# A hand-searched TensorE order is replaced, with longer planned landing times for two kinds of DMA

## Chip, cores and metric

The kernel runs on one core of one Trainium2 chip. The metric is device time in microseconds (us), taken for the whole program; lower is better. Engines are named as in the profile: PE (TensorE matmul), PEld (its weight loads), DVE (VectorE), ACT (ScalarE), POOL (GpSimd) and SP (SyncE, which here only issues DMAs).

## The reference

Two transformer-like layers in a row, each an attention block with a carried memory and a gated feed-forward block, with layer norms without scale ahead of both. Sequence 2048, width 576, 32 heads of 128, segments of 32 tokens, 8 memory tokens, feed-forward width 4608:

```python
for s in range(64):                                  # segments, in order
    h = concat([mem, x[s*32:(s+1)*32]])              # 8 + 32 tokens
    q, k, v = h@Wq, h@Wk, h@Wv                       # 32 heads of 128
    p = softmax(mask(q@k.T * 128**-0.5))             # memory sees all, tokens causal
    o = concat_heads(p@v) @ Wo
    mem, out[s] = o[:8], o[8:]                       # memory carried to the next segment
x = x + A(layernorm(x)); x = x + (silu(n@w1) * (n@w3)) @ w2, n = layernorm(x)
```

The same weights serve both layers. All inputs are bf16.

## The kernel before, in words

The two layers run interleaved, the second `LAG = 8` segments behind the first (L29): step t works on segment t of layer 0 and segment t-8 of layer 1, so there are 72 steps, of which the first 8 and the last 8 have one layer only. A step has four groups g of eight heads. For a group, PE makes Q and K (two units `QK` with tails `QKt`), then scores (`SC`). DVE and ACT make the softmax (mask add, max, subtract, exp on ACT, sum, normalise) and leave the probabilities in a buffer `PB`. They have to be transposed: in two-layer steps a DMA does it (`TR`, L402; the issue is at L1046 to L1050, 112 partitions of 1,024 bf16, 224 times in all), in one-layer steps PE does it (L405, 64 times). The result is in `PTS`, of which there is **one buffer** (`"pts": 1`, L38). PE multiplies it with V (`PV`, L415), the result is copied out to `OT`, and PE multiplies that with Wo (`WO` with tail `WOt`). After the transposition POOL clears `PB` (`pbz`, L406). Eight of the outputs' columns are the memory that the next step's Q, K and V start from.

Between these, PE does the feed-forward block, four segments (128 rows) at a time: up projections `FF` with tails `FFt`, tanh and two multiplications on ACT and DVE, down projections `W2`. The weights of the up projections are loaded from HBM again for each such job, 256 columns at a time (`W13`, L503, four DMAs, 2 buffers), those of the down projections too (`W2l`, L504). All these loads and the transpositions are issued by SP, in one order.

Nothing is scheduled at run time. `make_nodes` (L232) lists 10,997 pieces of work (nodes) with a planned duration, a planned latency `lat` from its end until others may use its result, the buffers that it takes (`acq`) and gives back (`rel`). `plan` (L78) walks through them with a simulated clock, and the order in which it places them is the order of each engine's instructions. For PE the order is not found but given: `FIRST` (L201), `FOUR` (L210, four steps, repeated 11 times) and `LAST` (L214) are strings with one letter for each PE node (Q is `QK`, q its tail, S scores, T a transposition on PE, P `PV`, O and o `WO` and its tail, F and f `FF` and its tail, W and w the down projections of layer 0 and 1, V, G and X the value projections, a small letter their tail). For the rest (the order on DVE, ACT, POOL and SP, whether a copy is done by DVE or ACT, which buffer is taken) the simulated clock decides, so planned durations and latencies matter there. A transposition is planned with 1.27 us of a DMA queue and then `lat`. 

PE can be split into half-width columns or half-height rows; a tail of 64 rows of contraction is done as two row halves at a time. A node that may be done either way (mode `"full/col"`) takes the mode of its neighbours, and in column mode each of its matmuls is written as two of 64 columns (`mm`, L615), which run side by side. Where consecutive nodes have no mode in common, PE changes its mode; the plan counts about 0.1 us for that (L33 to L34).

Of the kernel before, what the change touches and what calls it, by code (L numbers as in the profile page):

```python
# [34 lines left out]
PE_LAT = 0.22  # L35
EW_LAT = 0.135
# [5 lines left out]
def role(t):  # L42

    return (t - LAG) % 2
# [33 lines left out]
def plan(nodes, pools, letters):  # L78


    for n in nodes:
        for d in n.deps:
            d.outs.append(n)
    kinds = {}
    for n in nodes:
        if n.eng == "PE":
            kinds.setdefault(KINDS[n.name], []).append(n)
    its = {k: iter(v) for k, v in kinds.items()}
    seq = [next(its[c]) for c in letters]
    assert len(seq) == sum(len(v) for v in kinds.values())  # L90
    free = {k: [0.0] * c for k, c in pools.items()}
    t_eng = {e: 0.0 for e in ("PE", "ACT", "DVE", "POOL", "DMA", "SWD")}
    ready = {e: [] for e in t_eng}
    both = []
    mode, run = [], []
    order = []

    def settle():
        for x in run:
            x.mode = mode[0]  # L100
        run.clear()
    at = 0

    def push(n):
        if n.eng != "PE":
            (both if n.eng == "AD" else ready[n.eng]).append(n)

    def est(e, n):
        t = max(t_eng[e], n.ready)
        need = {}  # L110
        for s in n.acq:
            if s.i is None:
                need[s.pool] = need.get(s.pool, 0) + 1
        for p, c in need.items():
            t = max(t, sorted(free[p])[c - 1])
        return t

    for n in nodes:
        if n.left == 0:
            push(n)  # L120
    while len(order) < len(nodes):
        best = None
        for e in t_eng:
            if e == "PE":
                cands = seq[at:at + 1] if at < len(seq) and seq[at].left == 0 else []
            else:
                cands = ready[e] + (both if e in ("ACT", "DVE") else [])
            if not cands:
                continue
            ests = [(est(e, n), n) for n in cands]  # L130
            t = min(x for x, _ in ests)
            if t >= NOW:
                continue
            if best is None or t < best[0]:
                best = (t, e, ests)
        if best is None:
            raise RuntimeError(f"the plan is stuck at {at}: {seq[at].name}")
        t, e, ests = best
        st, n = min((x for x in ests if x[0] <= t + 1e-9), key=lambda x: x[1].prio)
        dur = n.dur  # L140
        if isinstance(dur, tuple):
            dur = dur[0] if e == "ACT" else dur[1]
        if e == "PE":
            at += 1
            if not any(m in mode for m in n.mode):
                dur += SWITCHES.get(f"{mode[0]} {n.mode[0]}", SWITCH) if mode else SWITCH
                settle()
                mode = n.mode
            mode = [m for m in mode if m in n.mode]
            run.append(n)  # L150
        elif n.eng == "AD":
            both.remove(n)
        else:
            ready[e].remove(n)
        n.start, n.end, n.by = st, st + dur, e
        t_eng[e] = n.end
        for s in n.acq:
            if s.i is not None:
                continue
            f = free[s.pool]  # L160
            s.i = min((i for i in range(len(f)) if f[i] <= st + 1e-9), key=lambda i: f[i])
            f[s.i] = NOW
        for s in n.rel:
            s.users -= 1
            s.end = max(s.end, n.end + (PE_LAT if e == "PE" else EW_LAT))
            if s.users == 0:
                free[s.pool][s.i] = s.end
        for m in n.outs:
            m.ready = max(m.ready, n.end + (0.0 if m.eng == e == "PE" else n.lat))
            m.left -= 1  # L170
            if m.left == 0:
                push(m)
        order.append(n)
    settle()
    return order
# [20 lines left out]
def ewh(*ns):  # L196
# [2 lines left out]


FIRST = (  # L201
    "amqQqQQSqqQSqQTQQqqSqQSxXVvPTPTOPOoToPOOooQQqqqqQSQvqSQVqQQqQSTqSPTXPOTOPToxoPOOooQQqqqvaSVQQqqQSQqTQPSqQqOSoTPO"
    "TPTPOOoooQQQqqqqQSvSVqqqQQQTSQqPTSOPXTOPTxooPOOooQQpQqqVvqqSnQQSFfqFQqfqqQTQSPFTSfWPOOoofTFPFTOPofOoWQqqqqQQSQQS"
    "FFffqVvqqWQQSTFxqffQFPSXWTFfPOTOPoofTOPFOooWVqfqvQQFSQqqQFSQqfqQWTSQqfPFQTfqFPSOTWPOOFoTooffPFOoWQQqqqqQSvQVSFqf"
    "QqQWqqSQTQPTaOPbSOTxxoPXoTXPOOoovqqpQQQSnQFqfqVSFqfqQQQqSPfqFQfOPSWOPFoOfoFoPWOoFQfqqqQQSQfqFFSGqfgqQQQPWQfqqSFG"
    "SfggGPFOOPWoGogfOPFOooWQQqqfaFSVfqqFQQvqfFSQWQfqqFPSQQWqfOSPFFOoPoWOoffFPOoWQqqqqQQbSQGSQqqgqQQSQqgPGSOPGggOPGOo"
    "PooOoQqqqpQpQQSvqqQSnnVqffFFQQPSqfqFQFSPWwffOFOPwWooFPOOooFqffqQQQqqwWSFQQQqfqfFSGSgqqQQgPGwGPWSggfFOGPOwFPOOooo"
    "oWQqfqqQQQfqSFSVvqqfQQFFPWSfqqQwQFSPaffOwWFPOFOPWOwfooooFfqqQQWQqqSQQqqSbQGgqqSQQgPGSGPGggOPOwOPoooOo"
)
FOUR = (  # L210
    "QQppQqqqqQvVSnnSQFqqfqQQFSqffQPFwOSPWFoffPOFOWwPFOoooFfqfqQQQQqqSWGSFqqfgQQQPQgqqwSGSFPGffggFWGPOwOFPOOoooowVqfq"
    "vQQQQqfqWSFSFfqqqQQwWQFPfqfSFwQOPSWFoFPffOOWPwOoooFqqfQQWQSqqqQQaSbQQqgqqGSQgPGSGPGggOPOwOPoooOo"
)
LAST = (  # L214
    "QqqqpQQQSnpQQqqqVvSnSQfqFFPqfQOWPSwoFffOPFoOFPwOffWooFQQQqqqFQSqffqFQQqgSWGSQPwQqqgfGSFPFgfgGwOPOGOPWOffooooFQQq"
    "qqFSQQqqqVSvQQwWQSPFqfqQOWoPSwFFPffOOWPwOoooFvfqQQQqqqQSVSFfqqfQFQQqqSPWQwSOPVovWPOwOPoobOoXxvppVqqQQQqqSQQnSnqq"
    "QFQSTfqfqQPFSTOPFTOPWTOPwOooooFfqqfQQQSQQqqqVvTSQFQqffqqFSQPwTWPSFfOFTwPOTWPOOooooFqfqfQQQwSQqxvqfXVWSFQFTQfqqWP"
    "wQSTFQfqfqFPSOTwPWFOffOTFPwOoooWoFfqqvVQQQqfqSQWwSFFQfqqQQSTWPQqqOTSoPTOPwOToboPxOoXqqqQQQpSVvqqqQQnSQFTfSFQPfqq"
    "QOTSFfPwOTFPofTOPFOooowQQfqqqQSQFvfqqVSQFfqQQSqfqQTwPFSTFPOTfXxPOTwPOOooooFVqqfvQQQSQqfqqQSQFqqqQSQTwPFTSOPoffTO"
    "FPwTOPoofOoFQQvqqQSQqqVSQqqqQqQSTQPTSPFOOTffooPFTOPwOoopFffFwnwFffffFFFwFwfffFFFwfffFFwFwfffFFFwffFFwfffFFww"  # L220
)
ORDER = FIRST + FOUR * 11 + LAST

# [1 line left out]
class Opt:  # L225

    qk, qkt, sc, tr, pv, wo, wog, vm = 0.0079, -0.0342, 0.0268, 0.1447, 0.0406, 0.2653, 0.0725, 0.1407
# [4 lines left out]
def make_nodes(em, nseg, pools, o=Opt, dma_bw=230e3, load_bw=345e3):  # L232
# [4 lines left out]
    def node(*a, **k):  # L237
        n = Node(*a, **k)
        nodes.append(n)
        return n  # L240
# [5 lines left out]
    kb = lambda rows, cols: rows * cols * 2  # L246
# [108 lines left out]
    def step(t):  # L355
# [3 lines left out]
        e = role(t)  # L359
# [13 lines left out]
        for g in range(NG):  # L373
            qs, qe = [], []
            for u in (2 * g, 2 * g + 1):
# [4 lines left out]
                          prio=pq, mode="full", acq=[q] + b, name="QK")  # L380
                n = node("PE", 4 * mm80, em.qk_tail(t, u, b), deps=hx + hm + ([ld_h[u // 4]] if t == 0 else []), prio=pq + o.qkt, mode="row",
                         acq=[q] + b, name="QKt")
# [6 lines left out]
            s = banks(1)[0]  # L389
            sme = Slot("sme")  # L390
            pf = t + o.gstep * g
# [4 lines left out]
            pb = Slot("pb")  # L396
            d = node("DVE", dve(320) + 0.2, em.sm_sum(t, g, sme), deps=[c], prio=pf, name="sum")
            w = 0.168 * (4 - e if nl == 2 else 2) + nl * 320 / 960
            pbs = node("DVE", w, em.sm_pb(t, g, sme, pb), deps=[d], prio=pf, acq=[pb], rel=[sme], name="pb")
            pts = Slot("pts")  # L400
            if nl == 2:
                tr = node("DMA", 1.27, em.ptr_dma(t, g, pb, pts), deps=[pbs], prio=pf - 0.02, acq=[pts], name="TR", lat=2.0)  # L402
            else:
                bt = banks()
                tr = node("PE", 8 * mm80, em.ptr(t, g, pb, bt), deps=[pbs], prio=pf + o.tr, mode="full/col", acq=[pts] + bt, name="TR")  # L405
            node("POOL", 1.2, em.pb_zero(pb), deps=[tr], prio=pf, rel=[pb], name="pbz")  # L406
            pe_ = [tr] if nl == 2 else [node("AD", ew(4 * c80), em.pt_ev(t, g, m, bt[m], pts), deps=[tr], prio=pf, rel=[bt[m]], name="PTe") for m in (0, 1)]
            if paired(t):
# [6 lines left out]
                      prio=pf + o.pv, mode="full/col", acq=b + [ot], rel=[pts], name="PV")  # L415
# [44 lines left out]
    def job(j):  # L460
# [24 lines left out]
        def units(pps, at0, end):  # L485
            for at, pp in enumerate(pps, at0):
# [3 lines left out]
                for pr_ in (2 * pp, 2 * pp + 1):  # L490
                    prio = (s0 + 4 if end and not last else s0) + o.ff + (o.win if s0 + 4 < nst else o.last_win) * (2 * at + pr_ % 2) / NPR
                    if stays:
                        w13, w2 = kept[pr_]
                        ld = []
                        w2s.append(w2)
                    elif in_tail:
                        w13 = w2 = None
                        ld = tail[pp]
                    else:
                        keep = before_last and pp == npp - 1  # L500
                        w13, w2 = Slot("w13", users=2 + keep), Slot("w2", users=ne + keep)
                        kept[pr_] = w13, w2
                        ld = [node("DMA", kb(1152, 256) / dma_bw, em.load_w13(pr_, w13), prio=prio - 1, acq=[w13], lat=2.0, name="W13")]  # L503
                        lds.append(node("DMA", kb(256, 576) / dma_bw, em.load_w2(pr_, w2), prio=prio - 0.99, acq=[w2], lat=2.0, name="W2l"))  # L504
                        w2s.append(w2)
                    b = banks()
# [863 lines left out]
```

## Time and profile before

| | |
|---|---|
| three runs, us | 2661.4, 2663.74, 2654.18 (median 2661.4) |
| profiled execution, us | 2657.08, of which the span of the instructions is 2655.3 |
| granted PE clock, mean | 0.992 |
| DVE, ACT, POOL busy, us | 2042.0 (77%), 1226.3 (46%), 334.9 (13%) |
| bytes moved by DMA | 371.44 MB, mean 140 GB/s |

The span is made of three stretches by the strings of letters: `FIRST` with the start-up from 12.4 to 528.1 us, 11 periods of `FOUR` up to 2221.1 us, then `LAST`. The profile's idle time of an engine is the time between two of its instructions, and each is put down to the instruction or DMA whose semaphore ended it. "DMA PTS<-PB" is the transposition of the probabilities, "DMA W<-in_B_w_dram" a load of `W13`, "DMA W2C<-in_B_w_dram" one of `W2l`.

### The profile page before, as it was taken

What the parts mean: (1) busy time and instruction counts of PE and PEld (TensorE: products, weight loads), DVE (VectorE), ACT (ScalarE), POOL (GpSimd) and SP (SyncE); (2) the same over time, 40 slices, a digit from 0 to 9 for tenths busy, and PEclk for the clock granted to TensorE, in tenths of its full rate; (3) what the DMA queues carried; (4) which work ended last, traced back from release to release, by engine and by line L of the source; (5) the groups of instructions that cost most, each with busy time, mean ns of one, the idle gap of its engine ahead of it and who ended that gap; (6) DMA issues with size and microseconds to landing.
All of it is one profiled execution on the core that took longest, in us unless ns stands there. A gap on an engine that the chain in (4) does not pass through costs nothing.

```text
span 2655.3 us, 132788 instructions
## 1 busy us (share of the span) xinstructions
PE 2577.3 (97%) x58915; PEld 2226.7 (84%) x58915; DVE 2042.0 (77%) x5253; ACT 1226.3 (46%) x3636; POOL 334.9 (13%) x399
## 2 busy tenths in 40 slices
PE   5999999999999999999999999999999999999998
PEld 4788888888888888888888888888888888888887
DVE  4787787787787778778777787787878777787876
ACT  2555453443445444444544444454534435454453
POOL 1111110110111011011101101110110111011110
PEclk8999999999999999999999999999999999999999
DMA  9064745665665556556454645645464564454456
GB/s 322 4 175 126 194 104 147 126 136 146 128 141 109 142 133 146 139 125 155 117 135 118 161 128 133 158 117 132 116 154 126 134 162 103 127 124 129 128 167 227
DMA packets 683056, 371.44 MB, mean 140 GB/s; under 512 B 233736, under 2 KB 672656, under 8 KB 681840
## 3 DMA queue, kind: packets, MB, share of 16 engines
q1 hardware_dynamic: 678944, 355.07, 52.9%
q8 instruction: 460, 7.54, 1.2%
q0 software_dynamic: 3024, 6.93, 0.9%
q10 hardware_dynamic: 512, 0.94, 0.2%
q14 instruction: 116, 0.95, 0.1%
HBM read 306.72 MB, written 2.36 MB: 116 GB/s over the span
## 4 chain that ended last, share of the span: by engine, by line
PE 83%; DMA 8%; DVE 5%; issue 1%; ACT 1%; SPq 1%; POOL 0%; ACTq 0%; DVEq 0%; POOLq 0%
PE bank L620 83%; DMA PTS<-PB 6%; DVE V L626 1%; DVE STAT L626 1%; DMA W<-in_B_w_dram 1%; DVE HTT L626 1%; DVE PB L626 1%; DVE SME L626 1%; DMA W<-in_A_Wk_dram 1%; SPq L629 1%; DMA W2C<-in_B_w_dram 1%; POOL PB L1041 0%; DMA WV<-in_A_Wv_dram 0%; DVE XR L626 0%; ACT V L623 0%
## 5 line engine op out<-in xcount | busy, mean ns | idle before, releaser
L620 PEld LDWEIGHTS <-W 128*128 128x128 bf16 (+2 forms) x31872 | 1254.5, 100 | 138.0 <-issue 68.5
L620 PE MATMUL bank<-HT,W 128*128 128x80 bf16 (+3 forms) x23040 | 804.6, 197 | 23.1 <-DMA W<-in_A_Wk_dram 8.7
L620 PE MATMUL bank<-XTB,W 128*64 128x256 bf16 (+5 forms) x8832 | 666.8, 263 | 2.5 <-DMA W<-in_B_w_dram 2.0
L1041 POOL MEMSET PB<- 128x1024 bf16 x288 | 274.1, 952 | 1954.7 <-DMA PTS<-PB 1298.5
L623 ACT ACTIVATE QKT<-bank 128x256 bf16<-128x256 f32 (+4 forms) x1546 | 356.3, 315 | 298.1 <-PE bank L620 287.2
L620 PE MATMUL bank<-OT,WO 128*128 128x80 bf16 (+3 forms) x11520 | 413.8, 198 | 1.2 <-ACT OT L623 0.6
L620 PEld LDWEIGHTS <-WO 128*128 128x128 bf16 (+1 forms) x11520 | 385.2, 102 | 26.4 <-issue 13.5
L623 ACT ACTIVATE V<-bank 64x512 bf16<-64x512 f32 (+1 forms) x583 | 328.9, 584 | 129.7 <-PE bank L620 122.5
L620 PE MATMUL bank<-WV,HT 128*32 128x512 bf16 (+3 forms) x3952 | 376.4, 386 | 1.2 <-DVE HT L626 0.7
L620 PE MATMUL bank<-W2C,HTT 128*64 128x288 bf16 (+1 forms) x3032 | 319.1, 287 | 1.3 <-DMA W2C<-in_B_w_dram 1.1
L623 ACT ACTIVATE HTT<-bank 128x512 bf16<-128x512 f32 (+1 forms) x324 | 175.7, 551 | 274.6 <-PE bank L620 273.4
L623 ACT ACTIVATE OT<-bank 128x320 bf16<-128x320 f32 (+1 forms) x378 | 142.2, 402 | 314.9 <-PE bank L620 312.1
L626 DVE TENSOR_REDUCE STAT<-SME 104x8 f32<-104x320 f32 (+1 forms) x576 | 273.6, 475 | 15.7 <-ACT SME L623 9.6
L626 DVE TENSOR_TENSOR PB<-SME,STAT 40x128 bf16<-40x128 f32 (+4 forms) x912 | 274.9, 335 | 11.0 <-DVE STAT L626 0.7
L620 PEld LDWEIGHTS <-HT 128*32 128x32 bf16 (+3 forms) x3952 | 168.3, 102 | 116.5 <-issue 22.1
L626 DVE SCALAR_TENSOR_TENSOR HTT<-HTT,bank 128x512 bf16<-128x512 bf16 (+1 forms) x324 | 202.0, 624 | 77.7 <-ACT HTT L623 74.5
L620 PEld LDWEIGHTS <-HTT 128*64 128x64 bf16 (+1 forms) x3112 | 227.8, 104 | 38.5 <-issue 3.4
L626 DVE SCALAR_TENSOR_TENSOR XR<-bank,XR 128x288 f32<-128x288 f32 x576 | 244.8, 448 | 18.5 <-PE bank L620 14.1
L626 DVE TENSOR_TENSOR HTT<-HTT,bank 128x512 bf16<-128x512 bf16 (+1 forms) x324 | 203.6, 628 | 30.8 <-DVE HTT L626 0.9
L626 DVE CAST V<-bank 64x512 bf16<-64x512 f32 (+1 forms) x281 | 192.2, 684 | 42.7 <-PE bank L620 36.3
L623 ACT ACTIVATE SME<-SME 104x320 f32<-104x320 f32 (+1 forms) x288 | 135.0, 469 | 148.1 <-DVE SME L626 146.4
L626 DVE CAST QKT<-bank 128x192 bf16<-128x192 f32 (+2 forms) x502 | 136.1, 315 | 75.3 <-PE bank L620 73.4
(58 smaller groups left out, 1426.2 us busy)
## 6 DMA issues: line engine op xcount, KB each, us to landing
W<-in_B_w_dram SPq DMA_DIRECT2D x608, 256.0 KB, 3.6
W2C<-in_B_w_dram SPq DMA_DIRECT2D x304, 288.0 KB, 3.5
W<-in_B_w_dram SPq DMA_DIRECT2D x608, 32.0 KB, 3.8
W<-in_B_w_dram SPq DMA_DIRECT2D x8, 1024.0 KB, 13.1
W<-in_A_Wq_dram SPq DMA_DIRECT2D x9, 512.0 KB, 9.2
WO<-in_A_Wo_dram SPq DMA_DIRECT2D x4, 1152.0 KB, 16.7
XR<-in_A_x_dram POOLq DMA_DIRECT2D x16, 288.0 KB, 3.8
WV<-in_B_w_dram SPq DMA_DIRECT2D x4, 1152.0 KB, 9.3
```

The lines of the kernel that those rows point to most:

```text
L620: self.ch("PE", self.nc.tensor.matmul(out, lhsT=lhsT, rhs=rhs, start=start, stop=stop, skip_group_check=True, **k))
L623: self.ch("ACT", self.nc.scalar.activation(*a, **k))
L626: self.ch("DVE", getattr(self.nc.vector, fn_)(*a, **k))
L629: self.ch("SP", self.nc.sync.dma_start(out=out, in_=in_))
L1041: return lambda n: self.ch("POOL", self.nc.gpsimd.memset(self.T.PB[:, pb.i], 0.0))
```

## The change

The three strings are replaced. The kinds of PE nodes and their number stay the same; their order changes. Two planned latencies are longer, and `plan` takes another time at which a buffer that a DMA node gives back is free:

```diff
         for s in n.rel:
             s.users -= 1
-            s.end = max(s.end, n.end + (PE_LAT if e == "PE" else EW_LAT))
+            s.end = max(s.end, n.end + (PE_LAT if e == "PE" else n.lat if e == "DMA" else EW_LAT))
...
-                tr = node("DMA", 1.27, em.ptr_dma(t, g, pb, pts), deps=[pbs], prio=pf - 0.02, acq=[pts], name="TR", lat=2.0)
+                tr = node("DMA", 1.27, em.ptr_dma(t, g, pb, pts), deps=[pbs], prio=pf - 0.02, acq=[pts], name="TR", lat=2.45)
...
-                        ld = [node("DMA", kb(1152, 256) / dma_bw, em.load_w13(pr_, w13), prio=prio - 1, acq=[w13], lat=2.0, name="W13")]
+                        ld = [node("DMA", kb(1152, 256) / dma_bw, em.load_w13(pr_, w13), prio=prio - 1, acq=[w13], lat=2.8, name="W13")]
```

The string of the repeated four steps, before and after (`FIRST` and `LAST` change in the same manner; the first 78 letters of `LAST` stay):

```diff
 FOUR = (
-    "QQppQqqqqQvVSnnSQFqqfqQQFSqffQPFwOSPWFoffPOFOWwPFOoooFfqfqQQQQqqSWGSFqqfgQQQPQgqqwSGSFPGffggFWGPOwOFPOOoooowVqfq"
-    "vQQQQqfqWSFSFfqqqQQwWQFPfqfSFwQOPSWFoFPffOOWPwOoooFqqfQQWQSqqqQQaSbQQgqqGSQgPGSGPGggOPOwOPoooOo"
+    "QqqqqQppQQVvSSnnQqfFQqfFSQQqfqPFOWoPSwFffOPFOwowoWPFOoFfqfQQQQqqqwSWFSGfqgqQQQPQgqqWSSGFPFffggGGPwOOFPOOffWooooFv"
+    "VqqqQQQwSFfqqqQQSwWFSPFfqfqQQOwSPoWFFPffOOwPWOoooFfqqqQWqSaQQQbSQqgqGSQPQqqgGOSPGggoOPGwOPooOo"
 )
```

More of the change, by code (lines that the diff above doesn't have):

```diff
@@ L201 @@
 FIRST = (
[L202 to L206, printed above, removed]
@@ L207 @@
-    "PooOoQqqqpQpQQSvqqQSnnVqffFFQQPSqfqFQFSPWwffOFOPwWooFPOOooFqffqQQQqqwWSFQQQqfqfFSGSgqqQQgPGwGPWSggfFOGPOwFPOOooo"
-    "oWQqfqqQQQfqSFSVvqqfQQFFPWSfqqQwQFSPaffOwWFPOFOPWOwfooooFfqqQQWQqqSQQqqSbQGgqqSQQgPGSGPGggOPOwOPoooOo"
+    "maqQQQqqQqSQQqSqqSqQQTSXxVvPTOPTOPTooOPOooQQqqqqQSQVvSqqQqQQqQTSSPTXPOTOPToxoPOOooQQqqvaSVqqQQQSQTqqqQSPQqTSPOTO"
+    "PTOPoooOoQQQqqqqQSvSVqqQqQQTSQqPTSOPXTOPTxooPOOooQQpvqVqqqQSnQFSfQFqqqfQTQQPSFfqTOSPWFTOoPffFTOPWOoooQQqqqqQSQFS"
+    "FQqfvfVQqqWQTSFPqfTQFPfSWTXxfPOFTOPOOfFooooWVvqqQQQfqqSFQFQSqfqQWTQSqfPFTQqPFSfWTOPOFOoTooffPFOoWQqqqqQQSvQVSfFQ"
@@ L209 @@
+    "qqQWqSQTQPTqOPSbaOoTXPoxTOPxoOoXvpQqqqQQSnQFqfVSQFqfqQQPqSFfqQFSPWOOPooffOWFPoOoFQQqqfQqfqFSWQQqqfgQSFGSGPQFqqgf"
+    "QOPoSGgfWOPFFfgGOPWOoooFQqfqfQQSFQqqfWFSvVFfqqQQQSPqWqQffPSFOaoOPWFOFPoofOoWQQqqqqQSQQbSQqqgqGSQPQqgGSOPgGGPOOog"
+    "oPoOoQqqqppQQQSvqqQnSnVqffFQFPSQQqfqFWFPwSOOffPooFOwFPWOooFffqqQQwQSWQFqqqfQQSFfqqgGSQPQqgWGSwPFfgfgGGPFOOPOOooo"
+    "owQWFQqfqfFSvVqqQwQQWSFqfqqQQPSWfqFQOPSwFFPoffOOWPwOoooFfqqqQQWqSaQQQbSQqgqGSQPQgqqGOSPGgGPgOwOPoooOo"
 )
 FOUR = (
-    "QQppQqqqqQvVSnnSQFqqfqQQFSqffQPFwOSPWFoffPOFOWwPFOoooFfqfqQQQQqqSWGSFqqfgQQQPQgqqwSGSFPGffggFWGPOwOFPOOoooowVqfq"
@@ L212 @@
-    "vQQQQqfqWSFSFfqqqQQwWQFPfqfSFwQOPSWFoFPffOOWPwOoooFqqfQQWQSqqqQQaSbQQqgqqGSQgPGSGPGggOPOwOPoooOo"
+    "QqqqqQppQQVvSSnnQqfFQqfFSQQqfqPFOWoPSwFffOPFOowoWPFOoFfqfQQQQqqqwSWFSGfqgqQQQPQqgqWSSGFPFffggGGPwOOFPOOffWooooFv"
+    "VqqqQQQwSFfqqqQQQSwWFSPFfqfqQQOwSPoWFFPffOOwPWOoooFfqqqQQWqSaQQQbSQqgqGSQPQqqgGOSPGggoOPGwOPooOo"
 )
 LAST = (
-    "QqqqpQQQSnpQQqqqVvSnSQfqFFPqfQOWPSwoFffOPFoOFPwOffWooFQQQqqqFQSqffqFQQqgSWGSQPwQqqgfGSFPFgfgGwOPOGOPWOffooooFQQq"
-    "qqFSQQqqqVSvQQwWQSPFqfqQOWoPSwFFPffOOWPwOoooFvfqQQQqqqQSVSFfqqfQFQQqqSPWQwSOPVovWPOwOPoobOoXxvppVqqQQQqqSQQnSnqq"
@@ L217 @@
[L217 to L220, printed above, removed]
+    "QqqqpQQQSnpQQqqqVvSnSQfqFFPqfQOWPSwoFffOPFoOFPwOffWooFQQQqqqFQSqffqFQQqgSWGSQPQwqqgfGSFPFgfgGwOPOGOPWOffooooFQQq"
@@ new lines @@
+    "qqFSQQqqqVSvQwQWQSPFqfqQOWoPSwFFPffOOWPwOoooFvqqQQQqfqQSVSFfqqfQFQQqqSPWQwSOPVvWPwoOOPoobOoXxvppVqqQQQSqqQQnSnqq"
+    "QFSTqfQQPfqFSTOPFTOPWTOPwOooooFfqfqQQQSQQvqqqVSTFQQqfqfqFSPQWwTSFfOPFTWPOTOPwOooooFfqfqQQQSQxvqqXVFwWSQTffqqFQPw"
+    "SWTQPQFfqfqFOTwSPWFOffOTFPwOoooWoFfqqvVQQQqfqSQWwSFFQfqqQQSTWPQqqOTSoPTOPwOToboPxOoXqqqQQQpSVvqqqQQnSQFTfSFQPfqq"
+    "QOTSoPfFOTwPFTOPoofOoFQQqqqfQQSFvqfqVwSQFfqQQTSfqqFPQTwSFPOTfxXPOTOPFOoooowVvfqQQqqQSQqQSQqfqFqqTQSQPwOTSFPoffTO"
+    "FPwTOPOoooFQqqfqQQSQvqqqVSQQQSqQqfTwPSTOPFTFPOOTffooPFoOopfwFnwFffffFFFwFFfwffFFwffFFwffFFwfffFFwFwFffffFFww"
```

## The prediction

> **What bounds the kernel now.** I read the page's first part, its chain, PE's waits, then single waits. PE is the bound: it is busy for 97% of the span, and no other engine for more than 77%.
>
> ```profile
> PE 2577.3 (97%) x58915; PEld 2226.7 (84%) x58915; DVE 2042.0 (77%) x5253; ACT 1226.3 (46%) x3636; POOL 334.9 (13%) x399
> ...
> PE 83%; DMA 8%; DVE 5%; issue 1%; ACT 1%; SPq 1%; POOL 0%; ACTq 0%; DVEq 0%; POOLq 0%
> ```
>
> The chain gives 8% to DMAs, but a chain is followed back over the whole landing of a transfer, while PE worked for most of it. What PE lost is in the list of waits:
>
> ```profile
> PE bank L620 <- DMA PTS<-PB: 19.9, 29, 1.5
> ...
> PE bank L620 <- DMA W<-in_A_Wk_dram: 8.7, 8, 1.3
> ...
> PE bank L620 <- ACT HT L623: 7.3, 18, 1.6
> ...
> PE bank L620 <- DMA W<-in_B_w_dram: 2.0, 5, 1.0
> ```
>
> The columns are us in total, times, longest. The transpositions are the largest: 15.5 of the 19.9 us lie in the 11 periods, 3.5 in FIRST, 0.9 in LAST. Wk belongs to the start-up. This list counts from the modelled end of a matmul. Counted from when the next could have started (the usual distance of starts), the 224 PVs behind transpositions lost 27.2 us.
>
> One wait shows how. SP's issues, then the chain of waits over it:
>
> ```profile
> 1163.62 2.28 SPq L629 DMA_DIRECT2D W<-in_B_w_dram  x4
> 1166.19 1.24 SPq L1050 DMA_TRANSPOSE PTS<-PB  x1
> 1167.53 1.04 SPq L629 DMA_DIRECT2D W2C<-in_B_w_dram  x2
> 1168.62 2.89 SPq L629 DMA_DIRECT2D W<-in_B_w_dram  x4
> ```
> ```profile
> 1166.19 4.82 DMA PTS<-PB
> 1171.01 0.04 issue
> 1171.06 8.96 PE bank L620 x141
> ```
>
> The last matmul of the PV before started at 1165.91; 0.28 us later, with PTS free, the transposition was issued. It took 4.82 us among weight loads. PE had 3.47 us of other work, and waited 1.6. All transpositions:
>
> ```profile
> DMA to landing us min/median/max: 2.9/3.2/5.2
> ```
>
> The upper quartile is 3.73 us. With no load issued from 2.5 us before to 1.5 us after, the median is 2.94 (58 of them); with 600 KB or more, 3.92 (23).
>
> **The change part by part.** *The free-time rule* does nothing: none of the nodes on the planned DMA queue gives a buffer back (PTS is given back by PV, PB by POOL, W13 by FF; stores are on the other queue). Cost 0, from the code alone, and no wait is added by it.
>
> *The two latencies* move no PE instruction, since its order is the strings'. They change what the simulated clock does on the other engines. ACT's listed order has 59 rows fewer; 55 copies of Q and K more go to DVE (334, before 279), 35 copies of V fewer (VGe 102, before 137). At 315 ns a Q or K piece (two a copy) and 684 ns a V copy that is at most 55 x 2 x 0.315 - 35 x 0.684 = +11 us for DVE in the span, about 0.5% of its load, hidden by its 23% idle time, unless it falls into a softmax: then at most the 11 us come on the path, at least 0. I take 0. On SP 304 W13 loads, 304 W2 loads and 224 transpositions stay; transpositions with a load right ahead fall from 170 to 171, that is, not; right behind, from 181 to 171. POOL's clears keep their order. So the traffic next to a transposition, its cause of lateness, stays.
>
> *More mode changes.* Counting the strings' nodes with their modes: 1,155 mode changes before, 1,238 after: FIRST +11, each period +6 (59 to 65), LAST +6. Starts of consecutive matmuls give the price: full after full 36 ns (1,202 node boundaries, median), row after full 134 (187), column after full 132 (181), full after row 131 (245) against 33 for row after row. So 0.097 us each: 83 x 0.097 = **+8.0 us**, on PE, with nothing to hide it. The order has 868 matmuls more, all halves of column mode; they run in pairs: an FF node takes 1.73 us in columns and 1.75 in full, W2 0.96 and 0.98, VG 1.73 both, PV 0.28 both. I take 0.
>
> *The distances.* I lay the trace's node durations (without waits) along both strings, and measure how much PE work stands between one PV and the next (the time for PTS to be filled again), and between a group's scores and its PV. Of the 224:
>
> | PE work from PV to PV, us | before | waited, us | after |
> |---|---|---|---|
> | under 3.5 | 41 | 14.5 | 4 |
> | 3.5 to 4 | 26 | 2.9 | 39 |
> | 4 to 6 | 61 | 7.1 | 85 |
> | over 6 | 96 | 2.7 | 96 |
>
> At the mean wait of each class of before (in quarter-us steps below 4) the new counts give 18.7 us, **8.5 less**. The other measure says less: scores to PV has 12 groups under 8.5 us, where there were 2, and its classes give 28.7 us, 1.5 more. So the ends are a saving of all 27.2 and a loss of 1.5. Going by place: the third group of steps 32, 36 ... 56 had 3.47 us to the PV before and 10.4 to its scores, and lost 7.1 us in 7 places; it gets 4.73 and 12.73: a landing as at 1166 (4.82 + 0.28) would then cost 0.4, not 1.6. Groups of steps 54 to 59, 15 and 19 with 6.6 us get a longer distance by one measure or the other; I give them 4. Against that, the last group of every fourth step has 8.39 us from its scores, and scores to landing took 8.5 (5% of all) to 9.5 (25%): 0.1 to 1.1 us for 12 groups that lost 2.5 before. I take no change there, and -10 us in all.
>
> By a rule of the Trainium skill (DMA: Bandwidth & Descriptors, sections "Anatomy of one DMA" and "Latency and other measured facts") a DMA has about 2.0 us of fixed cost and a transposition moves up to 261 GB/s; 229 KB here is then, as an estimate from that page, 2.9 us. The trace's undisturbed 2.94 agrees; by it alone the old plan of 1.27 + 2.0 had enough already, nothing would be saved, and the sum would be the +8.0; the trace's upper quartile of 3.73 speaks for the change.
>
> *Longer W13 loads.* PE's waits on W and W2C after the start-up were 2.0 and 1.1 us. At best 3.1 saved, at worst as much again lost. I take -1.
>
> *Others.* The waits on HT (one per period, 0.41 us) stay: the distance of 0.1 us is in both strings. Tails of Q and K come as soon as 1.34 us after the last WOt, before 1.83; the chain over ACT and DVE took 1.15 from that WOt, so 0. Copies of V before a PV have 1.48 us, before 1.89, and a copy takes 0.58 to 0.68: up to 0.3 us in 22 places; I take +1. The start-up waits for weights to about 59 us in either order: 0.
>
> **Sum**: +8.0 - 10 - 1 + 1 = -2 us on the profiled execution's 2657.08: **2655 us**. That execution is 4 us under the median of the three runs, which spread over 9.6; the forecast is no change that can be measured.
>
> **Rivals.** *A, the waits go.* With every PTS wait above 0.3 us a place gone (29 places, -24) and loads never late (-3), the sum is +8 - 24 - 3 = -19: **2638**. For it: the 41 short distances fall to 4. Against it: the traffic beside the transpositions stays, and 5 to 6 us of distance still lost 4.3 us in 8 of 27 places.
>
> *B, only the mode changes show.* If the waits move from PTS to the softmax, as the distance from scores measures it, +8 stays: **2665**, within 0.5%. The page's figures would end here too. Against it: the seven third groups gain on both measures.
>
> *C, slower: the softmax chain takes over.* In the last group of every fourth step and in others near 9 us, DVE (five of the chain's steps) is late, by the extra copies or by their new place. Price: scores to landing at the 50% row of 10.3 us against 8.39 is 1.9 us in 12 groups, 23 us; with 8 for mode changes and 10 saved at the other places, +21: **2678**. It decides from a mean of 9.8 us in these groups on (12 x 1.4 + 8 - 10 = 15). For it: 77% DVE and copies moved to it. Against it: with little distance the chain has hurried, since its order is planned around that: at 8.99 us (step 34) there was no wait.
>
> *D, the change doesn't do what it says*: true of the rule for free buffers, which moves nothing, and priced above.
>
> **Numbers.** Forecast 0.47, A 0.27, B 0.14, C 0.12. The measurement tells 0.5% (13 us) from no change. Faster by over 0.5% is A: 0.27; slower is C with 0.03 of B's edge: 0.15; the rest 0.58. The range goes from just below A, 2635, to 2673, short of C's price and past B's; the unknown ends (-27 to +1.5, -3 to +3, 0 to +11) fill it.
>
> **What would show it.** Right: the wait PE <- PTS at about 8 to 12 us, its third groups without waits, PE busy near 2585, periods at about 153.7 us (before: 153.9 on average, best 152.2). Wrong: PTS waits over 20 us (B or C; in C with the DVE write of PB ending within 3.3 us of PV), or under 4 (A); a busy time of PE that does not rise would say that mode changes are hidden; a landing median off 3.2 us, that SP's order changed the traffic.

## The result and the profile after

The changed kernel takes **2665.76 us** (median of 20 runs, 2660.23 to 2672.33), the kernel before, beside it, 2655.61 (20 runs): ratio 1.0036, 95% interval 1.0028 to 1.0045. So it is 10 us or 0.36% slower, where 2 us faster had been forecast. The number is nearly that of rival B (2665); whether B's reason is the right one is another question.

The profiled execution took 2666.47 us (span 2664.7). Its page, engines' busy time and the chain by engine:

```profile
PE 2589.4 (97%) x59783; PEld 2232.1 (84%) x59783; DVE 2024.0 (76%) x5276; ACT 1253.7 (47%) x3613; POOL 336.0 (13%) x399
...
PE 77%; DMA 5%; DVE 2%; issue 1%; ACT 1%; SPq 1%; POOL 0%; DVEq 0%; POOLq 0%; ACTq 0%
```

PE is still the bound; it is busy for 12.1 us more (2577.3 before) and has the 868 matmuls more that the strings give. The waits of PE in the same kernel (us in total, times, longest):

```profile
PE bank L620 <- issue: 14.5, 14, 3.8
PE bank L620 <- DMA PTS<-PB: 13.8, 22, 1.5
PE bank L620 <- DMA XTB<-in_A_mem_dram: 10.1, 1, 10.1
PE bank L620 <- ACT HT L623: 7.9, 19, 1.9
PE bank L620 <- DMA W<-in_A_Wk_dram: 6.8, 5, 2.6
...
PE bank L620 <- DMA W<-in_B_w_dram: 2.3, 6, 0.9
PE bank L620 <- DMA W2C<-in_B_w_dram: 1.9, 3, 0.9
```

The waits for transpositions did fall, 19.9 to 13.8 us (in the periods 15.5 to 7.5, in FIRST up from 3.5 to 5.4). "Issue", where PE waits for nothing that the profile shows, rose from 8.2 to 14.5; in before it was

```profile
PE bank L620 <- issue: 8.2, 9, 2.9
```

The landing of the transpositions in the kernel after:

```profile
DMA to landing us min/median/max: 2.9/3.1/5.1
```

It is as before (2.9/3.2/5.2). To see where the 10 us lie I cut each span at the first weight load of FOUR and of LAST (weight loads are counted, none is missing in these traces; the ends at 528.1 and 2221.1 us that were given for before ahead are 1.6 to 1.7 us later than this mark):

| us, profiled | to the end of FIRST | FOUR x 11 | LAST to the end | span |
|---|---|---|---|---|
| before | 526.5 | 1692.9 | 435.9 | 2655.3 |
| after | 530.6 | 1689.6 | 444.6 | 2664.7 |

The repeated part became 3.3 us shorter (153.6 us a period, 153.7 had been named as the sign), FIRST 4.1 longer, LAST 8.7 longer. That is one execution of each, and single executions scatter: that of e7 below took 2651.44 us where the median of its kernel is 2661.10.

### The profile page after: what moved, and what is told of

Read it like the earlier page. It is cut to its first block, busy times and chain, and to the rows that moved or that the text cites. A ratio compares the mean times of both kernels' runs of the same rounds, so it can differ in the third digit from the quotient of the medians.

```text
span 2664.7 us, 134355 instructions
## 1 busy us (share of the span) xinstructions
PE 2589.4 (97%) x59783; PEld 2232.1 (84%) x59783; DVE 2024.0 (76%) x5276; ACT 1253.7 (47%) x3613; POOL 336.0 (13%) x399
## 4 chain that ended last, share of the span: by engine, by line
PE 77%; DMA 5%; DVE 2%; issue 1%; ACT 1%; SPq 1%; POOL 0%; DVEq 0%; POOLq 0%; ACTq 0%
PE bank L620 77%; DMA PTS<-PB 4%; DMA W<-in_B_w_dram 1%; DVE STAT L626 0%; DVE V L626 0%; DVE PB L626 0%; DMA W2C<-in_B_w_dram 0%; SPq L1050 0%; DVE SME L626 0%; DVE XR L626 0%; DVE QKT L626 0%; SPq L629 0%; DVE LNS L626 0%; ACT V L623 0%; ACT QKT L623 0%
## 5 line engine op out<-in xcount | busy, mean ns | idle before, releaser
L620 PEld LDWEIGHTS <-W 128*128 128x128 bf16 (+2 forms) x32608 | 1272.0, 101 | 127.3 <-issue 59.7
L623 ACT ACTIVATE QKT<-bank 128x64 bf16<-128x64 f32 (+4 forms) x1440 | 335.6, 310 | 287.1 <-PE bank L620 277.6
L620 PE MATMUL bank<-OT,WO 128*128 128x80 bf16 (+2 forms) x11520 | 418.4, 199 | 6.9 <-issue 5.7
L623 ACT ACTIVATE V<-bank 64x512 bf16<-64x512 f32 (+1 forms) x628 | 353.4, 585 | 122.8 <-PE bank L620 115.6
L620 PE MATMUL bank<-WV,HT 128*32 128x512 bf16 (+4 forms) x3680 | 370.3, 385 | 0.4 <-issue 0.3
L620 PEld LDWEIGHTS <-HT 128*32 128x32 bf16 (+4 forms) x3680 | 159.5, 100 | 135.5 <-issue 31.5
L626 DVE CAST QKT<-bank 128x128 bf16<-128x128 f32 (+2 forms) x608 | 162.7, 315 | 99.8 <-PE bank L620 97.2
L626 DVE CAST V<-bank 32x512 bf16<-32x512 f32 (+1 forms) x236 | 161.4, 684 | 35.2 <-PE bank L620 31.5
```

Source lines behind the costliest of these rows:

```text
L620: self.ch("PE", self.nc.tensor.matmul(out, lhsT=lhsT, rhs=rhs, start=start, stop=stop, skip_group_check=True, **k))
L623: self.ch("ACT", self.nc.scalar.activation(*a, **k))
L626: self.ch("DVE", getattr(self.nc.vector, fn_)(*a, **k))
```

## The experiments

Verdicts are ratios of timed runs to the kernel before on the same chip. "New" and "old" strings are those after and before the change.

**e1 to e4, the parts.** All have the new latencies and the new rule; e1 has the new `FIRST`, e2 the new `FOUR`, e3 the new `LAST`, the other strings old; e4 has old strings only. What e4 keeps of the change:

```diff
-                tr = node("DMA", 1.27, ..., name="TR", lat=2.0)
+                tr = node("DMA", 1.27, ..., name="TR", lat=2.45)
...
-                        ld = [node("DMA", ..., lat=2.0, name="W13")]
+                        ld = [node("DMA", ..., lat=2.8, name="W13")]
```

> The new FIRST string, with FOUR and LAST of before, and the new latencies. Theory by place (the profiles of before and after differ by +4 us in FIRST, -3 in the periods, +9 in LAST and the end, since waits were removed in the periods alone): +4 us on before. Rival (the loss is the 83 mode changes wherever they stand, 0.097 us each, and the waits' sum stays): 11 of the changes are here, +1 us.

Measured: 2665.48, ratio 1.0042 (1.0028 to 1.0056).

> The new FOUR string, with FIRST and LAST of before, and the new latencies. Theory by place: -3 us on before (66 mode changes cost 6.4, waits for transpositions give back 9.6). Rival (mode changes alone): +6 us.

Measured: 2659.68, 1.0016 (1.0007 to 1.0026).

> The new LAST string, with FIRST and FOUR of before, and the new latencies. Theory by place: +8 us on before, with PE's idle time put down to issue in the last 100 us of the span near 9.5 us (before 6.1). Rival (mode changes alone, 6 of them here): +0.6 us, idle time as before.

Measured: 2659.74, 1.0018 (1.0007 to 1.0028).

> The two longer latencies and the free-time rule, with all three strings of before: PE's order is that of before. Theory by place: 0 +- 2 us, and PE's wait for transpositions stays near 20 us. Rival (the other engines' new order is what costs): +5 us or more.

Measured: 2656.69, 1.0008 (0.9999 to 1.0018).

The latencies and the rule cost nothing that can be told, 0 to 5 us. e1, e2 and e3, each one new string with the latencies, cost 10.7, 4.9 and 4.9 us (medians less 2654.82), where +4, -3 and +8 had been expected: all three expectations by place missed. Less the 1.9 us of e4 in each they are 15 us together, where the whole change costs 8 by the same count. The parts don't seem to add up (each ratio is good to some 3 us), as if something were at work that belongs to none of them. e1 also hints at it: it changes nothing in FOUR and yet is as slow as the whole.

**e5, the price of a mode change.** The order of before, with three PVs a period forced to column mode between neighbours of the full mode:

```diff
+            k = at - len(FIRST)
+            if 0 <= k < 11 * len(FOUR) and k % len(FOUR) in (30, 76, 100):
+                em.mode = "col"
```

> Before, with 33 PVs of the periods (three in each) written in column mode between neighbours in full mode: 66 mode changes more, every engine's order as before. Theory: a mode change is on PE and nothing hides it, so 66 x 0.097 = +6.4 us, all of it in the periods. Rival (PE's waits nearby become shorter by as much): 0 to +2 us.

Measured: 2662.34, 1.0021 (1.0012 to 1.0030), that is +5.6 us (3.2 to 8.0) for 66 mode changes, where 66 x 0.097 is 6.4. Its page and its wait for transpositions:

```profile
PE 2584.0 (97%) x59160; PEld 2230.2 (84%) x59179; DVE 2042.4 (77%) x5253; ACT 1226.9 (46%) x3636; POOL 334.7 (13%) x399
```
```profile
PE bank L620 <- DMA PTS<-PB: 17.8, 29, 1.4
```

PE is busy for 6.7 us more than in before (of 59,179 matmuls 19 are not in the trace), and the wait fell by 2.1 only. By the busy time the price stands. The timed 5.6 us agree with it, but prove less: each period has 24 matmuls more here, which moves the instruction fetches that e12 to e18 are about.

**e6 and e7, the large loads near the end.** In the last steps eight large loads of weights (20 DMAs of up to 1,152 KB) come in. Here they load 16 of 128 partitions, in the old (e6) and the new kernel (e7), so the last segments are computed with wrong weights.

```diff
-  self.dma(t13[:, 4 * kind:4 * kind + 4], wd[0:4 * P, fa:fa + 1024].rearrange(...))
+  self.dma(t13[0:16, 4 * kind:4 * kind + 4], wd[0:4 * P, fa:fa + 1024].rearrange(...)[0:16])
...
-  self.dma(t2, self.a.w2[fa:fa + 1024, :].rearrange(...))
+  self.dma(t2[0:16], self.a.w2[fa:fa + 1024, :].rearrange(...)[0:16])
```

> Before, with the eight big weight loads at the end reduced to 16 of their 128 partitions (the last down and up projections then work on wrong weights). Theory (PE's idle time put down to issue near 2590 to 2605 us is its instructions arriving late beside these loads): that idle time of 6.1 us goes to under 1, and the time falls by 5 to 6 us. Rival (those waits have another cause): no change.

Measured: 2652.39, 0.9990 (0.9982 to 0.9999).

> After, with the same eight loads reduced to 16 of 128 partitions (weights of the last job wrong). Theory: the idle time put down to issue in the last 130 us, 11.2 us, goes to under 1, and the time falls by 9 to 10 us, so that after and before with small tail loads are 6 to 7 us apart (before 10). Rival: no change, still 10 apart.

Measured: 2661.10, 1.0018 (1.0007 to 1.0029).

Each became 3 to 5 us faster, so the two are still 8.7 us apart by their medians (7.4 by the ratios): the loads explain some 1.4 to 2.2 of the 10 us, within what these runs can tell. (In the profiles they matter more for the new kernel: its issue waits in LAST fall from 11.5 to 2.4 us, those of the old from 6.3 to 2.5. The timed runs decide.)

**e8, the start.** The new kernel with the first 41 letters of the old `FIRST`:

```diff
-    "maqQQQqqQqSQQqSqqSqQQTSXxVvPTOPTOPTooOPO...
+    "amqQqQQSqqQSqQTQQqqSqQSxXVvPTPTOPOoToPOO...
```

> After, with the first 41 letters (step 0, while the weights arrive) of before. Theory by place: step 0 ends 1 to 1.5 us earlier, as in before, and the time falls by as much; the rest of FIRST stays. Rival (the start does not count, since the next steps wait for loads anyway): no change in the end of FIRST.

Measured: 2664.39, 1.0033 (1.0022 to 1.0044). In the profile step 0 ended 1.6 us sooner than in after, as expected; the whole gained 0.8 to 1.4, less than this measurement tells. The start isn't the cause.

**e9 and e10, the weight traffic.** After the first load of each buffer, W13 and W2 loads are cut to 16 of 128 partitions (stale weights are multiplied), in the old (e9) and the new kernel (e10):

```diff
+            r = 16 if ("w13", w13.i) in self.tail_w else P
-                self.dma(W[:, 4 * kind:4 * kind + 4], wd[0:4 * P, fa:fa + 2 * P].rearrange(...))
+                self.dma(W[0:r, 4 * kind:4 * kind + 4], wd[0:4 * P, fa:fa + 2 * P].rearrange(...)[0:r])
...
```

The rows of 64 and the W2 loads are cut in the same manner.

> Before, with the up and down projections' weight loads reduced to 16 of 128 partitions after each buffer's first (the feed-forward works on stale weights). Theory (transpositions are late because of the weight traffic): their median goes from 3.2 to about 2.95 us and the longest under 4, PE's waits for them in the periods (9.6 to 15.5 us in five profiles with the old FOUR) to under 4, and the time falls by 12 to 18 us. Rival (late for another reason, such as SP's order or the softmax): waits and time stay within 5 us.

Measured: 2644.28, 0.9927 (0.9913 to 0.9940), with the wait of its profile:

```profile
PE bank L620 <- DMA PTS<-PB: 24.2, 29, 1.7
```

> After, with the same loads reduced. Theory: here the waits in the periods go from 7 to under 3 us, so the time falls by 6 to 10 us only, and after stands 14 to 18 us over before, since the 83 mode changes stay (8 us) and there is little left that longer distances save. Rival (the longer distances are worth nothing in any case): both fall by the same, and stay 10 us apart.

Measured: 2651.41, 0.9955 (0.9941 to 0.9970), and

```profile
PE bank L620 <- DMA PTS<-PB: 15.2, 16, 1.9
```

The kernels get 19 and, from 1.0036 to 0.9955, 22 us faster, but not where I had said: the waits for transpositions rose a little in both (19.9 to 24.2, 13.8 to 15.2). Where the 19 us lie I did not follow further; the profiles show 9.8 of them (this chip's runs of the kernel before are some 8 us longer than those of the others, and it has no profile of before), 3.4 in FIRST, 2.8 in the periods, 3.7 in LAST. They are not waits: PE was not busy for 78.0 us of the span in before and 78.6 in e9, while its busy time went from 2577.3 to 2566.9. **My explanation of late transpositions by weight loads fell here.** The two are still 7.1 us apart.

So I looked for what else runs beside a late transposition. The kernel before, third part of its page (queue, kind: packets, MB, share of the DMA engines' time):

```profile
q8 instruction: 460, 7.54, 1.2%
```

7.54 MB in 460 packets is 16.4 KB each, and 58,915 matmuls over 460 is one packet per 128 matmuls with their weight loads (after: 467 for 59,783). So I read these packets as TensorE's instructions, fetched by DMA, and the place of a fetch is a place in the order of matmuls, not in time. The transposition of the prediction's example, issued at 1166.19, had one such fetch in its 4.82 us, at 2.77 us. A transposition raises its semaphore in sixteen steps, and in the trace fifteen of them had come by 3.26 us and the last at 4.82. The DMA view of that stretch:

```profile
q1 hardware_dynamic: 2065, 1.09, 88.2%
q8 instruction: 1, 0.02, 1.2%
```

One, two and three periods later the same transposition took 4.69, 4.70 and 4.56 us, with a fetch at 2.68, 2.51 and 2.13 us: a period of before has 3,330 matmuls, 26.02 fetches, so the same groups are hit period after period (a period of after has 3,410, 26.64, and every third repeats). Over all profiles of this study, with one fetch near and none of another engine:

| fetch starts, us after the transposition's issue | count | landing: quarter, median, three quarters |
|---|---|---|
| none near | 514 | 2.93, 2.97, 3.00 |
| -1.5 to 0 | 614 | 2.91, 2.95, 3.02 |
| 0 to 0.4 | 367 | 2.97, 3.17, 3.31 |
| 0.4 to 0.8 | 388 | 3.33, 3.45, 3.65 |
| 0.8 to 1.2 | 288 | 3.83, 4.01, 4.22 |
| 1.2 to 1.6 | 103 | 4.08, 4.30, 4.53 |
| 1.6 to 2.0 | 64 | 4.37, 4.49, 4.59 |
| 2.0 to 2.4 | 278 | 2.98, 4.40, 4.57 |
| 2.4 to 2.8 | 293 | 2.97, 4.55, 4.70 |
| 2.8 to 4.4 | 409 | 2.91, 2.94, 2.98 |

Transpositions with a fetch in their run land later, by up to 1.6 us in the medians; one that comes when they have landed does nothing. From 2.0 us on, at least a quarter of them are not late at all (2.98). This is a coincidence counted over traces; e12 to e18 below move it on purpose. In e9, with 1/8 of this weight traffic, it is the same: 52 transpositions with a fetch at 0.8 to 2.8 us have a median of 4.42, 140 with none from 0 to 2.8 us 2.91.

**e11, the new strings with the old latencies.** That is the change without the two `lat` and without the rule.

> The three new strings with the old latencies. Theory (the strings make the time; the latencies alone gave +2 +- 2.5): within 3 us of after, so +8 to +12 us on before. Rival (new strings need the other engines' order planned with long latencies): +15 us or more.

Measured: 2672.37 (before on this chip 2663.45), 1.0035 (1.0022 to 1.0047): the strings alone cost all of it.

**e12 to e18, the place of the fetches.** If it is a cause, then a few more matmuls at the start-up, where PE waits for weights anyway, move every later fetch to another place in an order that is otherwise the same, and 128 of them, a whole fetch, move it back onto itself. The added ones are 8 columns wide and their results are not used (60, 128, 32, 96 in the kernel before, 24, 56, 88 in the one after):

```diff
+            for _ in range(60):
+                self.mm(self.bk(b)[:, 256:264], self.T.ident[:, 0:P], self.T.ident[:, 0:8], True, True)
```

> Before, with 60 small matmuls (8 columns, result unused) behind the first one of the start-up, where PE waits some 6 us for weights. All else keeps its order. Theory (a transposition is late when one of PE's instruction fetches, one for each 128 matmuls, falls 0.2 to 2.8 us behind its issue): each later fetch comes 60 matmuls earlier in the work, and laying the shifted fetches on the trace of before gives 37 us of waits for transpositions where unshifted ones give 23: +10 to +14 us. Rival (fetches have nothing to do with it): 0 to +2 us.

Measured: 2663.38, 1.0031 (1.0019 to 1.0043). Two of its waits, which were 19.9 and 1.1 us in before:

```profile
PE bank L620 <- DMA PTS<-PB: 24.8, 34, 1.7
...
PE bank L620 <- DMA W2C<-in_B_w_dram: 4.7, 8, 1.4
```

> The same with 128 small matmuls, a whole fetch. Theory: the fetches fall where they fell, so the time is that of before within 2 us, and the late transpositions are those of before. Rival (the matmuls themselves cost time): twice what 60 cost.

Measured: 2655.39, 1.0000 (0.9990 to 1.0010), with

```profile
PE bank L620 <- DMA PTS<-PB: 17.9, 30, 1.4
```

> The same with 32 small matmuls. Theory: the shifted fetches give 24 us of waits: within 3 us of before. Rival (the matmuls themselves cost time): half of what 60 cost.

Measured: 2661.29, 1.0025 (1.0013 to 1.0037). I had expected within 3 us; it is 5.5 to 6.6.

> After, with 24 small matmuls in the same place. Theory: 20 us of waits where unshifted fetches give 10, so +5 to +10 us on after, +15 to +20 on before. Rival (longer distances keep any late landing hidden): after's time within 2 us.

Measured: 2661.12, 1.0019 (1.0009 to 1.0029): some 5 us *faster* than the changed kernel, where I had expected slower. My model, which moved the fetches of one trace along and added up the lateness, can't forecast the sign; it has the size.

> The changed kernel with 56 small unused matmuls at the start-up, so that every later instruction fetch comes 56 matmuls sooner in the order. At offsets 0 and 24 it was 10 and 5 us above the kernel before. If the order itself costs its 8 us of mode changes less some 6 of waits and the rest of the loss is the place of the fetches, offsets differ by 5 to 8 us and this one may come out as low as 1 to 3 us above the kernel before (2657 to 2659). If the loss is the order's own (mode changes and the softmax chain), it stays at 6 to 12 us above (2662 to 2668).

Measured: 2660.26, 1.0016 (1.0007 to 1.0025), 4.2 us above: between the two expectations.

> The same with 88 matmuls, the fourth offset of about a quarter of a fetch. Mean of the four offsets of the changed kernel: by the place of the fetches at most 5 us above the mean of the four offsets of the kernel before (which is some 4 us above its own time as it stands); by the order's own cost 8 or more above that mean.

Measured: 2659.44, 1.0009 (1.0001 to 1.0018).

> The kernel before with 96 small unused matmuls at the start-up. At 32 and 60 it lost 5 and 7 us, at 128 nothing. If the place of the fetches is what costs, this offset too lies above the kernel as it stands, by 0 to 8 us, or it shows that about half of all offsets are as good as the one it has. If the added matmuls themselves cost time, it would be some 10 us.

Measured: 2658.69, 1.0010 (1.0001 to 1.0019).

In the kernel before, a hundred and twenty-eight matmuls cost nothing and 60 cost 8 us (+10 to +14 had been expected): it isn't the matmuls, it is where they put the fetches. In e12 the two waits shown rose by 4.9 + 3.6 = 8.5 us, which is the whole loss (8.7 between the two profiles, and 8.5 longer periods).

The traces also show it transposition by transposition. From before to e12, 53 of the 224 lose a fetch at 0.8 to 2.8 us behind their issue, and their median landing goes from 4.09 to 3.03 us; 82 gain one, from 3.00 to 4.31; 88 have none in either, 3.04 and 2.99. With a whole fetch added (e13), 46 of the 54 that had one keep it, and stay at 4.20 and 4.29. So the fetch is the cause of the late landing.

All eight, with the wait for transpositions from each profile and the stages as in the first table:

| order, added | us over before (by ratio) | PTS waits, us | end of FIRST | FOUR x 11 | LAST |
|---|---|---|---|---|---|
| old, 0 | 0 | 19.9 | 526.5 | 1692.9 | 435.9 |
| old, 32 | 6.6 | 22.8 | 527.0 | 1699.0 | 432.7 |
| old, 60 | 8.2 | 24.8 | 528.9 | 1701.4 | 433.7 |
| old, 96 | 2.7 | 25.8 | 528.6 | 1696.2 | 437.1 |
| **mean** | **4.4** | **23.3** | **527.8** | **1697.4** | **434.9** |
| new, 0 | 9.6 | 13.8 | 530.6 | 1689.6 | 444.6 |
| new, 24 | 5.0 | 10.4 | 522.3 | 1687.6 | 443.8 |
| new, 56 | 4.2 | 11.6 | 522.0 | 1694.5 | 441.7 |
| new, 88 | 2.4 | 13.1 | 527.8 | 1693.4 | 437.3 |
| **mean** | **5.3** | **12.2** | **525.7** | **1691.3** | **441.9** |

At the same place of the fetches, on average over four, the new order is 0.9 us slower than the old one; with intervals of some 2.6 us on each ratio that is 1 us give or take 2, for these four places. The kernel before has the best of its four, the changed one the worst of its four, so about 9 of the 10 us hang on the places that these two happen to have. For the old order's share, 4.4, the cause is shown: 128 added matmuls do nothing, and in e12 the waits rose as much as the time. For the new order's, 4.3, it is not: no run has 128 matmuls added to the kernel after, its waits for transpositions at its own place are but 1 to 3 us higher than at the other three, and in the profiles its gain lies in FIRST (8 us at 24 and 56) or LAST (7 us at 88), not in the periods. The waits for transpositions are lower in the new order at every place.

The eight profiles also let the sum be redone as a mean. From the old order to the new, PE's busy time goes from 2576.5 to 2584.0 us, 7.5 more, and the rest of the span from 83.5 to 74.8, 8.7 less (19 matmul records are missing in each shifted profile of the old order and 41 in each of the new, which count as idle).

## Why the prediction was wrong

- **The bound**: right. PE, in both.
- **The free-time rule and the latencies, 0**: right within what can be told (e4: 0 to 5 us; e11 without them is no better than the whole change). The working under it was not: the copies of Q, K and V moved with the strings (the latencies alone, e4, move 2 copies of Q and K to DVE, not 55), copies of other kinds moved the other way, and DVE's busy time fell by 18.0 us where up to +11 had been reckoned.
- **Mode changes, +8.0**: right. e5 gave 5.6 (3.2 to 8.0) for 66, expected 6.4, and its PE is busy 6.7 us longer. In the whole change PE's busy time rose by 12.1, 4 more than they give; as a mean of four profiles each it is 7.5. So the 4 belong to this pair. Up to 2.7 of them can be the granted clock, 0.9919 and 0.9909 as the means of the two traces; the rest stays open.
- **The distances, -10**: right as a mean, wrong for the case at hand. On the profiles shown it was -6.1, from 19.9 to 13.8, outside the 8 to 12 that I had set as the sign; over four places of the fetches it is 23.3 to 12.2, -11.1. The third groups of steps 32 to 56 lost their waits as foreseen; others got them, since every third period of after repeats its own pattern of fetches.
- **"So the traffic next to a transposition, its cause of lateness, stays"**: this step failed. Transpositions come late where a fetch of TensorE's instructions falls into them, with 1/8 of the weight traffic as with all of it (e9: 4.42 with a fetch, 2.91 without), and the place of these fetches does not stay when the order changes. I had carried the lateness of each class of distances from the old order to the new; of the classes' mean waits a part was the old order's own luck, and I gave that no price. It is worth 8 us from one place to another without any change in the order (e12), as much as the largest cost of the sum.
- **New waits, +1, start-up, 0, and FIRST and LAST by their mode changes alone**: the waits for copies of V did not grow (2.9 us before, 2.7 after). The start-up was 0.7 us longer in the two profiles, and as long on average (head of the order to its 41st node: 57.5 and 57.6 over the four places). FIRST is 2.0 shorter as a mean. LAST was mis-sized: 0.6 for six mode changes, +7.0 measured as a mean of four profiles, most of it in its last 65 us. The string is not all of it: with the old LAST and the new latencies (e1, e2, e4) LAST took 439.6 to 442.2 us in the profiles, against 432.7 to 437.8 with the old latencies (before, e12, e13, e14, e18); the new LAST with the old latencies (e11) took 442.8. At the end one-layer steps run matmuls of 40 columns, and PE waits for nothing that the profile names. The timeline of PE in the kernel after, start, length, and the wait in brackets:

```profile
2600.08 1.43 PE L620 MATMUL bank<-HT,W 128*128 128x40 bf16 x51 [1.95 <-issue]
2605.74 0.33 PE L620 MATMUL bank<-PTS,V 128*128 128x40 bf16 x7 [1.21 <-issue]
2612.03 1.36 PE L620 MATMUL bank<-OT,WO 128*128 128x40 bf16 x48 [1.46 <-issue]
2619.27 1.75 PE L620 MATMUL bank<-OT,WO 128*64 128x40 bf16 x48 [3.83 <-issue]
```

  In before the same stretch has three such waits, one of 1.36 us at 2589.81 and these:

```profile
2597.12 2.40 PE L620 MATMUL bank<-HT,W 64*128 64x40 bf16 x79 [2.90 <-issue]
2603.33 0.41 PE L620 MATMUL bank<-PTS,V 128*128 128x40 bf16 x7 [1.83 <-issue]
```

  In 2.4 us PE goes through 79 matmuls there, so a fetch of 128 lasts for some 4 us. The traces tell what PE waits for: its next instructions. In after the last six such waits stand at weight loads 58,541, 58,669, 58,797, 58,925, 59,052 and 59,179, that is a fetch apart, and in all twenty profiles the 103 waits of over 0.2 us put down to issue in LAST end 2.2 to 3.6 us (median 2.5) after a fetch started. Over the four places they make 5.1 us in the old order and 8.1 in the new, 3 of the 7.0. Why the fetches come too late just there is not shown: cutting the large loads beside them (e7) shortened LAST to 430.7 us in the profile, but the timed runs gained 4.8 us where the old kernel gained 2.7 (e6), a difference within their intervals.
- **W13 loads, -1**: not seen. W and W2C waits went from 3.1 to 4.2 us; e12 shows that these, too, depend on the place of the fetches (W2C 1.1 to 4.7).
- **Rival B** had the number, not the reason: the waits did not move from PTS to the softmax (the wait for `PB` is 1.9 us, 3 times). **C**: no. **A**: the traffic stayed, and so did a part of the waits. **D**: true of the rule.

What stays open: why the new order at its own place is 5 us slower than at the next three, though its waits for transpositions are but 1 to 3 us higher there (the added matmuls also let step 0 end 1.7 to 2.6 us sooner in their profiles; e8 tells that this alone gives little). One rival was not tested: the granted clock. Its mean over the timed runs is 0.9916 in the changed kernel and 0.9924, 0.9929 and 0.9932 with 24, 56 and 88 matmuls added; the kernel before has 0.9929. From run to run of one kernel 0.001 less goes with 0.7 us more (337 runs), and at most, if all of the clock counted, it would be 2.7; so the clock can be 1 to 3.5 of the 10 us, and whether the order causes it is not known. Open is also which of a hundred and twenty-eight places is best, which only a run can tell so far. No version beat the kernel before at full work: the nearest are the old order with a whole fetch added (1.0000) and with the new latencies (1.0008).

## What to carry to other kernels

Before a fraction of a percent is put down to an order, move the same order by a part of an instruction fetch (here by 32, 60 and 96 unused matmuls) and see how far that alone moves the time; a single difference smaller than that, here 8 us of 2656, says nothing about the order. A search that scores orders by their run times, or a reader who compares single traces, picks lucky places: compare means over several. And a wait of an operation that recurs at the same place in every period is a sign to count what else recurs there, the instruction fetches among it (3,330 matmuls to a period are 26.02 fetches).

## What the runs showed of the hardware

- TensorE's instructions come in fetches of 16.4 KB, one per 128 matmuls with their weight loads (460 for 58,915), and where a fetch starts 0.8 to 2.8 us after the issue of a DMA transposition of 229 KB, that lands at 4.05 to 4.42 us (medians of the twenty kernels) where 2.97 is the rule.
- The undisturbed 2.97 agrees with the 2.9 us that the prediction had estimated from the Trainium skill (DMA: Bandwidth & Descriptors, sections "Anatomy of one DMA" and "Latency and other measured facts"). In the same sections of the Trainium skill the 261 GB/s are the figure for a transposition with a non-contiguous middle dimension, not an upper bound (about 350 to 400 for a contiguous one), and the 2.0 us are a fit on DMAs that GpSimd issues, while SP issues these; so the agreement tells less than it seems to.
- PE can run out of instructions: 103 waits in LAST, up to 3.8 us each, end 2.2 to 3.6 us after a fetch started.
- Column mode doubles the instructions of a node: 868 matmuls more were 7 fetches more (460 to 467).
- Weight loads beside the transpositions hardly make them late: with 1/8 of the W13 and W2 traffic their landing without a fetch from 0 to 2.8 us went from 2.97 to 2.91 us, and PE's wait for them did not fall.
- A change of PE's mode costs some 0.1 us on PE and is not hidden (PE busy 6.7 us longer for 66, timed 5.6, interval 3.2 to 8.0; by the starts of matmuls 0.097).
